# The first layer of the routed experts: clipping and copying out of PSUM on ScalarE instead of VectorE

## Chip, core and metric

One core of a Trainium2 chip runs the whole program once. The metric is device microseconds of one execution. TensorE (PE in the rows) multiplies matrices and writes to PSUM; VectorE (DVE) and ScalarE (ACT) read PSUM; GpSimd (POOL) does elementwise work in SBUF and triggers indirect DMAs.

## What is computed

A decayed linear attention gives x of 3072 tokens by 512. Two dense layers follow. Then comes a mixture of eight experts with fixed capacity: a greedy routing gives every expert exactly 384 tokens, and each expert applies two matrices with a clip at zero between them.

```python
logits = x @ w_gate
flat = logits.flatten()
order = np.argsort(-flat)
...
for e in range(E):
    mask = assigned == e
    h = np.maximum(x[mask] @ w1[e], 0.0)
    out[mask] = h @ w2[e]
```

The change is about `np.maximum(x[mask] @ w1[e], 0.0)`, the expert's first layer.

## The kernel before

Matrices are split into two float16 parts, a high part and the rest, and a product is made of three matmuls (high by high, high by rest, rest by high). So a first-layer result is needed three times: in float32, rounded to float16 (the high part), and as the difference of the two (the rest).

The experts run one after the other in `expert(r)`, r from 0 to 7. The first layer has 8 groups (`f`); a group is 12 matmuls of 128x384 into one PSUM bank. The banks come in turn from `ps_any()`: two called `ph` and two called `px`, four in all, so a bank comes back after four groups. A group leaves PSUM by three instructions: L918 on VectorE scales, clips and writes the float32 copy `hs` (`HS2`, two buffers that lie in the tile `G_67`); L919 on ScalarE rounds `hs` to the high part in `hid` (in `G_68`); L920 on VectorE subtracts for the rest. The second layer follows, three pieces of 24 matmuls of 128x512 into the same banks, each copied out by L936 on ScalarE and scattered to the output by an indirect DMA of GpSimd (L937).

Beside experts 0 to 4 runs the routing, rounds 2 to 6, in `route_round(r)`. A round searches a threshold in five digits. One digit is a loop between two engines: VectorE compares (`against`, L686, result in `ld`), TensorE counts (L729, `pc2x6x` is round 2, step 6), VectorE tests (L731), TensorE sums over partitions (L734, `pn2x7x`), VectorE reduces (L736) and subtracts (L740), and the next compare follows. A round ends with L745, L747, L749, L750 and L751 on VectorE, for which the matmuls L776 (`pp2x10x`) wait. Also beside the experts, `weights(i)` prepares the next expert's matrices: GpSimd triggers the load (L862), ScalarE squares (L868) and writes the high part (L228 in `split`), VectorE writes the rest (L229), after a scale (`se`, L192 to L196) that VectorE makes.

The order on TensorE and ScalarE in this stage is that of the code, woven by a hand-made table of due times (`Weave`, `KN`). The order on VectorE and GpSimd is chosen when the program is built, by a scheduler that works with priorities; `tc.high_priority()` puts the three instructions of a group ahead of others that are ready.

Of the kernel before, what the change touches and what calls it, by code (L numbers as in the profile page):

```python
# [16 lines left out]
AF = mybir.ActivationFunctionType  # L17
OP = mybir.AluOpType
# [7 lines left out]
G = 384  # L26
# [72 lines left out]
def moe_kernel(ctx, tc, qkv, w_in, w_out, w_gate, w1p, w2p,  # L99
               c_mask, c_g, c_gv, c_gs, out, dbg=None):  # L100
    nc = tc.nc
    V, A, P, T, SY = nc.vector, nc.scalar, nc.gpsimd, nc.tensor, nc.sync
# [416 lines left out]
    def mm3(p, pairs, cost):  # L519
        n = len(pairs) * 3  # L520
        piece = PC[0]
        i = 0
        for (sh, sl), (mh, ml) in pairs:
            for a, b in ((sh, mh), (sh, ml), (sl, mh)):
                T.matmul(p, a, b, start=i == 0, stop=i == n - 1)  # L525
                i += 1
                if i % piece == 0 and i < n:
                    yield piece * cost
# [136 lines left out]
    def rt(name, shape, dt=F32, bufs=1):  # L665
        n = int(np.prod(shape))
        w = n if dt in (F32, I32) else (n + 1) // 2
        if name not in views:
            views[name] = []
            for _ in range(bufs):  # L670
                seg = next(x for x in segs if x[1] + w <= x[0].shape[1])
                v = seg[0][:, seg[1]:seg[1] + w]
                seg[1] += w
                v = v if dt == F32 else v.bitcast(dt)[:, :n]
                if len(shape) == 2:
                    v = v.rearrange("p (a b) -> p a b", b=shape[1])
                elif len(shape) == 3:
                    v = v.rearrange("p (a b c) -> p a b c", b=shape[1], c=shape[2])
                views[name].append(v)
        turns[name] = turns.get(name, -1) + 1  # L680
        return views[name][turns[name] % len(views[name])]
# [160 lines left out]
    def ps_any():  # L842
        return next(banks)()
# [63 lines left out]
    def expert(r):  # L907
        W, hid, idx, xt = EWB[r % 2], HID[r % 2], IDX[r], XTE_[r]
        for f in range(NF2):
            if f == 2:  # L910
                RUN.add(r)
            p = ps_any()
            yield from mm3(p[:, :G], [((W[:, 0, k * F + f * 128:k * F + (f + 1) * 128],
                                        W[:, 1, k * F + f * 128:k * F + (f + 1) * 128]),
                                       (xt[:, 0, k], xt[:, 1, k])) for k in range(KD)], 0.163)
            hs = HS2[f % 2]
            with tc.high_priority():
                V.tensor_scalar(hs, p[:, :G], 1.0 / 65536.0, 0.0, op0=OP.mult, op1=OP.max)  # L918
                A.activation(hid[:, 0, f], hs, AF.Copy)  # L919
                V.tensor_tensor(hid[:, 1, f], hs, hid[:, 0, f], op=OP.subtract)  # L920
            yield PC[0] * 0.163
        while r not in SC:
            yield 0.5
        fac = rt("fac", [CPG], bufs=3)
        for c in range(CPG):
            xg = XG[(r % 2) * CPG + c]
            V.tensor_scalar(fac[:, c:c + 1], xg[:, 2 * DM:2 * DM + 2].bitcast(F32), SC[r], None, op0=OP.mult)
        H2.add(r)
        for c in range(CPG):
            p = ps_any()  # L930
            yield from mm3(p, [((hid[:, 0, f, c * C:(c + 1) * C], hid[:, 1, f, c * C:(c + 1) * C]),
                                (W[:, 0, 4096 + f * DM:4096 + (f + 1) * DM], W[:, 1, 4096 + f * DM:4096 + (f + 1) * DM]))
                               for f in range(NF2)], 0.216)
            o = OUTR[(r * CPG + c) % 4]
            with tc.high_priority():
                A.activation(o, p, AF.Copy, scale=fac[:, c:c + 1])  # L936
            s = P.indirect_dma_start(out=out, out_offset=bass.IndirectOffsetOnAxis(ap=idx[:, c:c + 1], axis=0),  # L937
                                     in_=o, in_offset=None)
            for old in scat:
                tc.declare_no_dep(s.ins, old.ins, reason="rows of other tokens")  # L940
            scat.append(s)
            if c == CPG - 1:
                OUT.add(r)
            yield PC[0] * 0.216
# [209 lines left out]
    for r in range(E):  # L1154
        need(lambda: r in XTE and r in SPL)
        wv.run(expert(r))
# [57 lines left out]
```

## Time before, and its profile

| | |
|---|---|
| time, median of 3 runs | 1114.64 us (1114.42 to 1118.55) |
| profiled execution, its own time | 1124.75 us |
| span of that execution | 1123.0 us |
| mean granted TensorE clock | 0.942 |
| busy: PE / DVE / ACT / POOL | 973.1 / 811.1 / 625.3 / 415.1 us |

The span runs from the first to the last instruction of the profiled execution; 1.75 us of its own time lie around it. That execution took 10.1 us (0.9%) more than the median of the three others.

### The profile page before, as it was taken

How to read it: one execution, taken by the hardware profiler on the slowest of the kernel's cores; microseconds unless marked ns; L12 is line 12 of the kernel's file. 1: busy time of each engine (PE TensorE's matmuls, PEld its weight loads, DVE VectorE, ACT ScalarE, POOL GpSimd, SP SyncE). 2: the span in 40 equal slices, each digit the busy share in tenths (PEclk: the TensorE clock that was granted, in tenths of full speed). 3: DMA queues.
4: the chain of work that ended last, by engine and by line, in shares of the span. 5: the costliest groups of instructions: out<-in, count | busy, mean ns of one | idle time of the engine just before them, and what ended most of it. 6: DMA issues, size and time to landing. Idle time of an engine off the chain costs nothing.

```text
span 1123.0 us, 19760 instructions
## 1 busy us (share of the span) xinstructions
PE 973.1 (87%) x7897; PEld 559.5 (50%) x7897; DVE 811.1 (72%) x1815; ACT 625.3 (56%) x925; POOL 415.1 (37%) x301
## 2 busy tenths in 40 slices
PE   3448758898999999999999999997688887979997
PEld 2335434444655555556556555553444544545553
DVE  6899989953676687677767654578779887795641
ACT  4435867563477567567577468126345545455731
POOL 5956364551533463435544514100331211314111
PEclk9959889978999999999999999999699998999999
DMA  9461262156113122131234010062734735726500
GB/s 305 122 187 39 103 178 66 39 118 136 39 38 86 39 62 71 48 85 30 60 101 86 11 38 1 20 207 104 160 108 140 219 100 148 217 86 212 183 29 29
DMA packets 108813, 113.66 MB, mean 101 GB/s; under 512 B 92464, under 2 KB 92592, under 8 KB 106672
## 3 DMA queue, kind: packets, MB, share of 16 engines
q1 hardware_dynamic: 102576, 66.24, 23.3%
q0 software_dynamic: 6144, 46.15, 11.9%
q8 instruction: 62, 1.02, 0.4%
q14 instruction: 31, 0.25, 0.1%
HBM read 77.50 MB, written 13.64 MB: 81 GB/s over the span
## 4 chain that ended last, share of the span: by engine, by line
PE 48%; DVE 24%; issue 15%; POOL 6%; ACT 3%; DMA 2%; another core or an unknown queue 0%; POOLq 0%; SPq 0%; ACTq 0%; DVEq 0%
PE px L525 20%; PE ph L525 19%; DVE WOUT L229 2%; DVE WIN L229 2%; DVE ld L686 2%; PE py L434 2%; DVE RAW L571 1%; POOL out_dram L937 1%; DVE ld L373 1%; POOL amt L406 1%; DVE G L918 1%; DVE RAW L555 1%; PE pa L397 1%; DVE WOUT L249 1%; DMA xt<-yh 1%
## 5 line engine op out<-in xcount | busy, mean ns | idle before, releaser
L525 PE MATMUL ph<-xt,WIN 128*128 128x384 f16 x1728 | 331.1, 333 | 7.9 <-DVE RAW L555 3.6
L525 PE MATMUL px<-WOUT,G 128*128 128x512 f16 x1248 | 314.4, 387 | 0.6 <-DVE WOUT L229 0.6
L525 PEld LDWEIGHTS <-WIN 128*128 128x128 f16 x1920 | 186.4, 100 | 147.9 <-issue 22.4
L525 PEld LDWEIGHTS <-G 128*128 128x128 f16 x1728 | 166.7, 100 | 184.3 <-issue 18.3
L577 POOL TENSOR_TENSOR G<-RAW,G 128x1536 f16<-128x1536 f32 (+1 forms) x32 | 99.5, 3109 | 101.7 <-DVE G L574 88.8
L406 POOL TENSOR_TENSOR amt<-amt 128x512 f16<-128x512 f32 x40 | 55.7, 1394 | 124.4 <-DVE amt L403 108.2
L555 DVE TENSOR_SCALAR RAW<-ph 128x384 f32<-128x384 f32 x124 | 68.0, 550 | 42.0 <-PE ph L525 41.5
L562 ACT ACTIVATE RAW<-RAW,zt,ch 128x1536 f32<-128x1536 f32 x32 | 53.3, 1665 | 52.2 <-DVE RAW L555 48.2
L325 ACT ACTIVATE junk<-ld 128x512 bf16<-128x512 f32 x63 | 39.4, 626 | 62.0 <-DMA ld<-in_qkv_dram 61.1
L919 ACT ACTIVATE G<-G 128x384 f16<-128x384 f32 x64 | 33.0, 519 | 72.5 <-DVE G L918 72.4
L571 DVE TENSOR_TENSOR RAW<-RAW 128x1536 f32<-128x1536 f32 (+1 forms) x33 | 60.0, 1817 | 15.5 <-ACT RAW L570 15.4
L868 ACT ACTIVATE junk<-RAW 128x1024 bf16<-128x1024 f32 x64 | 67.1, 1048 | 6.1 <-DMA RAW<-in_w1p_dram,MASK 5.4
L862 POOL DMA_INDIRECT RAW<-in_w1p_dram,MASK x8 | 8.3, 1041 | 164.9 <-issue 55.2
L223 POOL TENSOR_TENSOR RAW<-ld,RAW 128x512 f16<-128x512 f32 x34 | 45.7, 1358 | 49.9 <-ACT RAW L222 45.0
L228 ACT ACTIVATE WOUT<-RAW,se 128x1024 f16<-128x1024 f32 x32 | 35.7, 1137 | 39.6 <-DVE se L195 39.6
L400 DVE TENSOR_TENSOR amt<-pa,MASK 128x512 f32<-128x512 f32 x38 | 26.1, 687 | 37.8 <-PE pa L399 33.4
L525 PEld LDWEIGHTS <-WOUT 128*128 128x128 f16 x384 | 37.7, 101 | 26.1 <-issue 3.7
L525 PE MATMUL px<-WIN,G 128*128 128x512 f16 x192 | 45.6, 389 | 2.9 <-ACT G L919 2.2
L570 ACT ACTIVATE RAW<-RAW 128x1536 f32<-128x1536 f32 (+1 forms) x33 | 47.7, 1445 | 0.4
L223 POOL TENSOR_TENSOR STH<-SC,STH 64x256 f16<-64x256 f32 x34 | 32.1, 945 | 41.7 <-ACT STH L222 38.7
L563 ACT ACTIVATE RAW<-RAW 128x1536 f32<-128x1536 f32 x32 | 47.2, 1475 | 0.3
L228 ACT ACTIVATE WIN<-RAW,se 128x1024 f16<-128x1024 f32 x32 | 35.7, 1137 | 17.1 <-DVE se L195 17.1
(582 smaller groups left out, 2002.8 us busy)
## 6 DMA issues: line engine op xcount, KB each, us to landing
ld<-in_qkv_dram SPq DMA_DIRECT2D x20, 768.0 KB, 4.9
G<-in_w_in_dram SPq DMA_DIRECT2D x8, 1024.0 KB, 7.2
G<-in_w_out_dram SPq DMA_DIRECT2D x8, 1024.0 KB, 5.4
x_rows<-xr SPq DMA_DIRECT2D x24, 256.5 KB, 2.9
G<-in_qkv_dram SPq DMA_DIRECT2D x2, 768.0 KB, 6.4
g_columns<-G SPq DMA_DIRECT2D x1, 1024.0 KB, 8.5
G<-g_columns SPq DMA_DIRECT2D x1, 1024.0 KB
ld<-in_qkv_dram SPq DMA_DIRECT2D x3, 256.0 KB, 4.2
```

The lines of the kernel that those rows point to most:

```text
L223: (V if pool in ("V", "E") else P).tensor_tensor(lo, src, hi, op=OP.subtract)
L228: A.activation(hi, src, AF.Copy, scale=s)
L229: V.scalar_tensor_tensor(lo, src, s, hi, op0=OP.mult, op1=OP.subtract)
L406: (P if mode[1] == "P" else V).tensor_tensor(amh[:, j, 1], am, amh[:, j, 0], op=OP.subtract)
L525: T.matmul(p, a, b, start=i == 0, stop=i == n - 1)
L555: V.tensor_scalar(hs[:, f], p[:, :G], 1.0 / 65536.0, None, op0=OP.mult)
L562: A.activation(th, hs, AF.Tanh, scale=ch[:, q:q + 1], bias=z)
L563: A.activation(th, th, AF.Arctan, scale=-0.5, bias=0.5)
L570: A.activation(th[:, w], th[:, w], AF.Sin, scale=-2.0, bias=math.pi / 2)
L571: (V if hm[1] == 'V' else P).tensor_tensor(th[:, w], th[:, w], hs[:, w], op=OP.mult)
L577: (P if lo == 'P' else V).tensor_tensor(gb[:, 1, o], th[:, w], gb[:, 0, o], op=OP.subtract)
L868: A.activation(junk(1024), RAW[:, o:o + 1024], AF.Square, accum_out=ss[:, j:j + 1])
```

## The change

The first of the three instructions moves from VectorE to ScalarE, and both of ScalarE's now read PSUM: L918 clips straight into the high part in float16, L919 clips once more into the float32 copy. VectorE keeps the subtraction.

```diff
             hs = HS2[f % 2]
             with tc.high_priority():
-                V.tensor_scalar(hs, p[:, :G], 1.0 / 65536.0, 0.0, op0=OP.mult, op1=OP.max)
-                A.activation(hid[:, 0, f], hs, AF.Copy)
+                A.activation(hid[:, 0, f], p[:, :G], AF.Relu, scale=1.0 / 65536.0)
+                A.activation(hs, p[:, :G], AF.Relu, scale=1.0 / 65536.0)
                 V.tensor_tensor(hid[:, 1, f], hs, hid[:, 0, f], op=OP.subtract)
```

On ScalarE the pair L918, L919 stands wherever L919 stood, 64 times, and nothing else moves; the number of table loads is 65 in both programs. TensorE and SyncE have the same rows as before. On GpSimd some output scatters (L937) change places with loads and gathers. VectorE loses 64 instructions, and the scheduler orders the others anew around them. Three places show how.

VectorE in round 2, beside expert 0's first layer, between two counts of TensorE; before (`G_67` holds `hs`, `G_68` holds `hid`):

```order
L731 TENSOR_SCALAR MASK<-pc2x6x 64x8
L229 SCALAR_TENSOR_TENSOR WOUT<-RAW,se_8832,WOUT 128x1024
L918 TENSOR_SCALAR G_67<-ph 128x384
L736 TENSOR_REDUCE MASK<-pn2x7x 128x1
L740 SCALAR_TENSOR_TENSOR MASK<-MASK 128x192
L918 TENSOR_SCALAR G_67<-px 128x384
L920 TENSOR_TENSOR G_68<-G_67,G_68 128x384
L686 TENSOR_TENSOR ld<-MASK,ld 128x24x64
L920 TENSOR_TENSOR G_68<-G_67,G_68 128x384
L731 TENSOR_SCALAR MASK<-pc2x8x 64x8
```

and now:

```order
L731 TENSOR_SCALAR MASK<-pc2x6x 64x8
L736 TENSOR_REDUCE MASK<-pn2x7x 128x1
L740 SCALAR_TENSOR_TENSOR MASK<-MASK 128x192
L686 TENSOR_TENSOR ld<-MASK,ld 128x24x64
L920 TENSOR_TENSOR G_68<-G_67,G_68 128x384 x2
L731 TENSOR_SCALAR MASK<-pc2x8x 64x8
```

The weight instruction L229 and both L918 have left the way to the compare L686; the subtractions L920 follow it. (An L229 stands further ahead now, before L736 of `pn2x5x`.)

VectorE at the end of round 5, beside expert 3's first layer, before:

```order
L736 TENSOR_REDUCE MASK<-pn5x9x 128x1
L920 TENSOR_TENSOR G_68<-G_67,G_68 128x384
L918 TENSOR_SCALAR G_67<-px 128x384
L745 SCALAR_TENSOR_TENSOR MASK<-pn5x9x,MASK,ld 128x8
L229 SCALAR_TENSOR_TENSOR WIN<-RAW,se_10461,WIN 128x1024
L918 TENSOR_SCALAR G_67<-ph 128x384
L920 TENSOR_TENSOR G_68<-G_67,G_68 128x384
L747 TENSOR_REDUCE MASK<-MASK 128x1
L229 SCALAR_TENSOR_TENSOR WIN<-RAW,se_10461,WIN 128x1024
L920 TENSOR_TENSOR G_68<-G_67,G_68 128x384
L749 TENSOR_SCALAR MASK<-MASK 128x24
```

and now:

```order
L736 TENSOR_REDUCE MASK<-pn5x9x 128x1
L229 SCALAR_TENSOR_TENSOR WIN<-RAW,se_10461,WIN 128x1024
L745 SCALAR_TENSOR_TENSOR MASK<-pn5x9x,MASK,ld 128x8
L920 TENSOR_TENSOR G_68<-G_67,G_68 128x384
L747 TENSOR_REDUCE MASK<-MASK 128x1
L229 SCALAR_TENSOR_TENSOR WIN<-RAW,se_10461,WIN 128x1024
L749 TENSOR_SCALAR MASK<-MASK 128x24
```

The two L918 are gone from this chain, and of three L920 one is left in it; both L229 have stayed.

VectorE in round 6, beside expert 4's first layer, before:

```order
L731 TENSOR_SCALAR MASK<-pc6x6x 64x8
L229 SCALAR_TENSOR_TENSOR WOUT<-RAW,se_10945,WOUT 128x1024
L736 TENSOR_REDUCE MASK<-pn6x7x 128x1
L920 TENSOR_TENSOR G_68<-G_67,G_68 128x384
L740 SCALAR_TENSOR_TENSOR MASK<-MASK 128x192
L918 TENSOR_SCALAR G_67<-px 128x384
L920 TENSOR_TENSOR G_68<-G_67,G_68 128x384
L686 TENSOR_TENSOR ld<-MASK,ld 128x24x64
```

and now:

```order
L731 TENSOR_SCALAR MASK<-pc6x6x 64x8
L229 SCALAR_TENSOR_TENSOR WOUT<-RAW,se_10945,WOUT 128x1024
L736 TENSOR_REDUCE MASK<-pn6x7x 128x1
L920 TENSOR_TENSOR G_68<-G_67,G_68 128x384
L740 SCALAR_TENSOR_TENSOR MASK<-MASK 128x192
L229 SCALAR_TENSOR_TENSOR WOUT<-RAW,se_10945,WOUT 128x1024
L920 TENSOR_TENSOR G_68<-G_67,G_68 128x384
L686 TENSOR_TENSOR ld<-MASK,ld 128x24x64
```

Here L918 is gone from ahead of the compare L686, but a second L229 has come in its place; it stood behind the compare before.

## Rows read from the trace of the kernel before

**Rows 1.** The page: busy time, share of the span and instructions of each engine.
```profile
PE 973.1 (87%) x7897; PEld 559.5 (50%) x7897; DVE 811.1 (72%) x1815; ACT 625.3 (56%) x925; POOL 415.1 (37%) x301
```

**Rows 2.** Stretches: length, busy PE, PEld, DVE, ACT, POOL; PEclk; DMA share, GB/s.
```profile
800.00:998.00 198.00, 173.45 (x1467) 95.53 (x1467) 165.00 (x501) 103.64 (x159) 38.91 (x34) 0.96 0.53 151
...
1014.00:1115.00 101.00, 100.86 (x566) 53.42 (x563) 47.85 (x90) 50.55 (x79) 18.97 (x18) 1.00 0.39 120
```

**Rows 3.** Waits of PE in 800 to 998: us, times, longest.
```profile
PE pp5x10x L776 <- DVE MASK L751: 2.8, 1, 2.8
...
PE pc5x4x L729 <- DVE ld L686: 2.4, 1, 2.4
PE pn4x5x L734 <- DVE MASK L731: 2.0, 1, 2.0
...
PE pc4x8x L729 <- DVE ld L686: 1.5, 1, 1.5
...
PE pc2x8x L729 <- DVE ld L686: 1.3, 1, 1.3
...
PE pp3x10x L776 <- DVE MASK L751: 1.0, 1, 1.0
...
PE pc3x6x L729 <- DVE ld L686: 0.3, 1, 0.3
```

**Rows 4.** PE in order of time, at the end of expert 4's first layer.
```profile
1004.96 0.66 PE L525 MATMUL px<-WIN,G 128*128 128x512 f16 x2 [2.20 <-ACT G L919]
```

**Rows 5.** Groups of DVE in 800 to 998: busy us, mean ns | idle before.
```profile
L229 DVE SCALAR_TENSOR_TENSOR WOUT<-RAW,se,WOUT 128x1024 f16<-128x1024 f32 x20 | 25.5, 1276 | 2.0 <-ACT WOUT L228 2.0
L920 DVE TENSOR_TENSOR G<-G,G 128x384 f16<-128x384 f32 x39 | 21.4, 550 | 0.3
...
L918 DVE TENSOR_SCALAR G<-px 128x384 f32<-128x384 f32 x20 | 11.0, 552 | 4.9 <-PE px L525 4.8
```

**Rows 6.** Groups of ACT in the same stretch.
```profile
L919 ACT ACTIVATE G<-G 128x384 f16<-128x384 f32 x39 | 20.3, 520 | 51.0 <-DVE G L918 50.9
```

**Rows 7.** Line L557 (an ACT copy from PSUM in an earlier phase): ns min/median/max.
```profile
L557 ACT ACTIVATE RAW<-ph x4: 471/491/492, 155.9 to 172.3; 128x384 f32<-128x384 f32 x4
```

**Rows 8.** DVE in order of time, expert 0's first layer, round 2.
```profile
813.58 0.54 DVE L918 TENSOR_SCALAR G<-ph 128x384 f32<-128x384 f32 x1
814.05 0.14 DVE L736 TENSOR_REDUCE MASK<-pn2x7x 128x1 f32<-128x8 f32 x1
...
815.54 0.55 DVE L920 TENSOR_TENSOR G<-G,G 128x384 f16<-128x384 f32 x1
816.01 0.95 DVE L686 TENSOR_TENSOR ld<-MASK,ld 128x1536 bf16<-128x1536 bf16 x1
```

**Rows 9.** DVE, end of round 5.
```profile
943.79 0.17 DVE L736 TENSOR_REDUCE MASK<-pn5x9x 128x1 f32<-128x8 f32 x1
...
947.50 1.27 DVE L229 SCALAR_TENSOR_TENSOR WIN<-RAW,se,WIN 128x1024 f16<-128x1024 f32 x1
...
949.60 0.24 DVE L751 SCALAR_TENSOR_TENSOR MASK<-MASK 128x24 bf16<-128x24 bf16 x1
```

**Rows 10.** ACT, expert 4's first layer.
```profile
980.35 1.15 ACT L228 ACTIVATE WOUT<-RAW,se 128x1024 f16<-128x1024 f32 x1 [3.68 <-DVE se L195]
981.41 0.51 ACT L919 ACTIVATE G<-G 128x384 f16<-128x384 f32 x1
981.82 1.13 ACT L228 ACTIVATE WOUT<-RAW,se 128x1024 f16<-128x1024 f32 x1
```

**Rows 11.** DVE, the same place: the compare that PE waits for.
```profile
984.64 0.95 DVE L686 TENSOR_TENSOR ld<-MASK,ld 128x1536 bf16<-128x1536 bf16 x1
```

**Rows 12.** Two stretches with a lower granted clock (columns as in rows 2).
```profile
950.00:954.00 4.00, 4.00 (x18) 1.99 (x17) 3.55 (x19) 1.47 (x3) 0.98 (x1) 0.60 0.31 55
1004.00:1015.00 11.00, 9.32 (x52) 3.92 (x53) 8.10 (x17) 6.79 (x10) 5.21 (x4) 0.69 0.21 48
```

**Rows 13.** PE, one group of expert 7, whose first layer runs undisturbed.
```profile
1085.51 2.11 PE L525 MATMUL px<-xt,WOUT 128*128 128x384 f16 x12
```

## The prediction

> **What bounds the kernel now.** I read the page first [rows 1]: TensorE is busy for 87% of the span, VectorE for 72%, ScalarE for 56%. A mean over the span says little of this change, which touches the eight experts alone, so I cut the expert stage with the view of stretches [rows 2]. From 1014 to 1115 us TensorE is busy for 100.86 of 101 us at full clock: nothing that another engine does faster can shorten that part, though TensorE could be made to wait anew. From 800 to 998 us, where the routing runs beside experts 0 to 4, TensorE is idle for 198.00 - 173.45 = 24.6 us, and VectorE is busy for 165 of 198. At 1004.96 TensorE waits another 2.2 us [rows 4]. So the change plays for at most some 27 us of idle TensorE, and for what a low clock costs after such waits.
>
> The waits say who makes TensorE idle [rows 3]. Nearly all of it is VectorE. Four waits are for L751, the end of a routing round, from 2.8 to 1.0 us, 8.0 in sum. Seven are for the compare L686 beside a first layer, from 1.5 to 0.3 us, 7.6 in sum. `pc5x4x` waits 2.4 us for a compare beside a second layer. The rest is short, with one exception: `pn4x5x` waits 2.0 us for a test (L731) that VectorE began late though it had nothing else to do. I cannot put that on VectorE's load, and leave it as it is.
>
> **The change, part by part.** *VectorE loses L918.* Each takes 0.55 us [rows 5]; the next instruction starts 0.47 us after it began (813.58 to 814.05) [rows 8], so each one gone frees 0.47 us of the queue. 40 of the 64 stand between 800 and 998 (the group with `px` is one half of them): 18.8 us of a queue that is busy for 165. The 24 behind stand where TensorE does not wait and are worth nothing.
>
> *ScalarE gains a read of PSUM.* The trace has the same shape with an immediate scale in line L557: 0.49 us [rows 7]; L919 from SBUF is 0.52 [rows 6]. One L919 begins and the next L228 follows 0.41 us later (981.41 to 981.82) [rows 10], so I take 0.39 us of the queue for each new one. A clip out of PSUM is not in ScalarE's rows. Bounds: 0.47, L557's shortest, and 0.55, what VectorE's clip takes; I take 0.49, the row with the same engine, source and shape. ScalarE's added time is 40 x 0.39 = 16 us in the stretch, on 103.64 of 198 busy.
>
> On this the Trainium skill speaks against the change: the page "ScalarE: Activation LUTs", section "Rules for kernel authors", sends relu and max to VectorE, as the engine that is faster per element. The rows differ for this shape, float32 out of PSUM: 0.55 us on VectorE against 0.49 on ScalarE. By the rule the move would cost more than it frees, and the time would be that of the first rival below.
>
> *ScalarE waits for TensorE instead of VectorE.* L919 waited 50.9 us in this stretch for L918 [rows 6]. Now the pair waits for the group's last matmul, and VectorE's queue no longer delays it. Behind it stand L228 and L868 of the next weights, which come a little earlier too. No table load is added (65 in both programs). The high part, which TensorE needs first, is written by the first of the two.
>
> *The queue of VectorE is ordered anew.* This decides the sum. I walked three places.
>
> Round 2, beside expert 0. Before, L736 started at 814.05 behind L918, and the compare at 816.01 behind L918 and L920 [rows 8]; the count after it waited 1.3 us [rows 3]. In the new order the two L918, the L920 and an L229 are gone from between: more than 1.3 us even of the three 0.47 alone. This wait goes: -1.3.
>
> End of round 5. From L736 at 943.79 to the end of L751 at 949.84 [rows 9] VectorE needs 6.05 us: 3 x 0.47 for L920, 2 x 0.47 for L918, 2 x 1.2 for L229, the rest for the short chain. TensorE was through 2.8 us before that, at 947.1. The new order has two L229 and one L920 between, four times 0.47 = 1.9 us less, and the idle time before an L918 goes: L751 ends near 947.8, and 0.7 of 2.8 us are left. -2.1.
>
> Round 6, beside expert 4. Here a second L229 comes ahead of the compare, against one L918 gone, and it has to wait for its L228. On ScalarE an L228 (1.06 us) and a pair (0.8, before 0.41) alternate [rows 10]; with the scale 0.4 sooner the third L228 ends near 984.8. L229 and L920 follow (1.2 + 0.47), and the compare starts near 986.6 instead of 984.64 [rows 11]. The wait grows by about 1.3, since the test before it is 0.7 late as well and holds TensorE there: +2.0 together.
>
> The others I walked the same way, without rows here. The four round ends lose 6.1 of their 8.0 us. Of the seven compares beside first layers four have one L229 more ahead of them in the new order, two the same number and one has one less: in sum -1.5 of 7.6 (bounds: -7.6 if all go, +5 if each of the four grows by one L229). `pc5x4x` has one L229 less: -1.2. The start of round 3 has one L918 less: -0.5. At 1004.96 TensorE waits 2.2 us [rows 4] for the high part of expert 4's last group, which stands on ScalarE behind an L228 that waits for VectorE's scale; VectorE is three L918 earlier there, and now writes nothing between: -1.4. Sum: -10.7 us.
>
> *The clock.* After such waits the granted clock is lower: 0.60 from 950 to 954, 0.69 from 1004 to 1015 [rows 12]. That costs 0.40 x 4.0 = 1.6 and 0.31 x 9.3 = 2.9 us of TensorE's time; over 800 to 998 the mean is 0.96 [rows 2], 0.04 x 173 = 6.9 us. Which of these vanish hangs on single microseconds. Bounds 0 and -9.8; I take a third, -3.
>
> *GpSimd's order.* Output scatters change places with loads; the gathers of an expert's tokens stand a whole expert ahead of their use in both orders, and that covers it. If the cover went, a gather's trigger would be late by one scatter, about a microsecond.
>
> *From 1014 on.* ScalarE has 50.55 us of work in 101 [rows 2]; 24 pairs add 9. A bank is needed again three groups later, and a group takes 2 us [rows 13], so a pair may be 6 us late before TensorE waits. By the walk it is 1 to 4 us late. Nothing.
>
> The sum on the profiled execution is 1124.75 - 13.7 = 1111.0. The median of the other runs is 10.1 us lower, so part of the waits in this trace are not in those runs, and my walks allow for no accidental stall. I carry 70% over: 1114.6 - 9.6 = **1105.0 us**.
>
> **Rivals.**
>
> *ScalarE gives the time back (about 1114 us).* L920 now comes after two instructions of ScalarE, each pair behind an L228 (1.06 us) or an L868. VectorE runs its rows in their order, so an L920 that waits for ScalarE holds the routing chain behind it. Before, this cost 0.3 us in the stretch [rows 5]. If each of 40 L920 waits 0.25 us more, 10 us are gone and no gain is left. For it: a pair is 0.4 us longer than L919. Against it: the pair begins sooner, by what the 50.9 us of waits for L918 were. This is where the rule of the Trainium skill named above would lead.
>
> *The new order makes it slower (about 1121 us).* The place in round 6 is the model: an L229 ahead of the compare costs 2 us there. If all four such places cost that (+8) and the round ends gain nothing, with two of them losing an L229's 1.2 (+2), against 3 to 4 us saved elsewhere, the sum is +6 or 7. It decides from the point where the L229 that moved ahead cost more than the freed 18.8 us of queue return on the path. For it: four of seven compares do get one more. Against it: the L918 that are gone, 0.47 us each, stood in the same stretches of the queue.
>
> *A bank comes late (about 1114 us).* ScalarE may stand at an L228 that waits for a scale, 3.68 us [rows 10], while the group in front of it is done. Before, VectorE emptied the bank meanwhile. In round 6 the lag becomes 3.3 us, under the 6 that are free. If it grew by another 5 at each of the five experts, stalls of 2 us would take the gain.
>
> *Everything falls into place (about 1096 us).* All waits for VectorE but the odd one go (-21), the clock stays up (-6), and 70% of it shows.
>
> **How the numbers follow.** What a measurement of this kernel can tell from no change is about 0.5%, 5.6 us: faster is below 1109.1, slower above 1120.2. The forecast has 0.55, everything in place 0.08, ScalarE giving it back 0.19, the late bank 0.05, the new order 0.13. Faster 0.63, same 0.24, slower 0.13. The range leaves out 0.08 below and 0.12 above: 1097 to 1117.
>
> **What would show it.** L918 as an instruction of ScalarE of about 0.49 us, and 40 instructions fewer on VectorE from 800 to 1000. TensorE idle in that stretch for about 14 us instead of 24.6. Waits for L751 of a microsecond or less; a longer wait of `pc6x8x`; the wait near 1005 at about 0.8. L920 idle for ScalarE under 3 us. The prediction is wrong if L920 waits 10 us or more for L919, if the compares wait longer in most rounds, or if TensorE waits for a bank that ScalarE has not read.

## The result, and the profile after

The changed kernel takes 1102.84 us in the median of 4 runs (1102.40 to 1103.25), beside 1114.53 us of the kernel before (4 runs, 1113.72 to 1118.55) on the same chip: a ratio of 0.989, 95% interval 0.987 to 0.991. In a second set of runs, on a chip where the kernel before took 1118.09 us, it was 1102.47 us, a ratio of 0.986 (0.981 to 0.990). The profiled execution took 1103.10 us, its span is 1101.3 us. Medians and ratios leave out executions more than 1.5% above the fastest of their kernel; only `free` below has such, four of twelve, and its profile is of one of them.

The page answers to [rows 1]. VectorE has 64 instructions fewer, ScalarE 64 more, and TensorE is busy for a little less time with the same matmuls:

```profile
PE 966.6 (88%) x7897; PEld 559.9 (51%) x7897; DVE 783.0 (71%) x1751; ACT 646.3 (59%) x989; POOL 416.8 (38%) x301
```

The stretches answer to [rows 2] (length, busy PE, PEld, DVE, ACT, POOL; PEclk; DMA share, GB/s). From 800 to 998 us TensorE is idle for 198.00 - 183.88 = 14.1 us, where it was 24.6. The two stretches do not hold the same work: the last L776 of the routing, that of round 7, starts at 980.5 us now, at 998.0 before, and the new stretch holds about 100 matmuls more. Up to that L776, from 800 to 980.5 us, TensorE is idle for 180.50 - 167.82 = 12.7 us. The undisturbed part begins earlier, and TensorE is still busy for all of it:

```profile
800.00:998.00 198.00, 183.88 (x1566) 101.78 (x1565) 163.08 (x511) 127.34 (x214) 51.57 (x40) 0.98 0.56 167
...
992.00:1093.00 101.00, 101.00 (x567) 53.59 (x565) 38.36 (x69) 58.38 (x104) 21.10 (x19) 1.00 0.39 123
```

The waits of PE from 795 to 1012 us (us, times, longest) answer to [rows 3]. Of four waits for L751 two are left, 2.0 us in sum; `pc5x4x` waits 0.2 us. Two compares wait clearly longer than they did: `pc6x8x`, 2.4 us instead of 1.3, with the test before it (`pn6x7x`, 0.8), and `pc6x2x`, 1.2 instead of 0.3. (The longest in this window, `pc2x2x`, lies ahead of 800 us; it is 4.4 us, 4.5 before.) Two rows of the kernel before, then the new waits:

```profile
PE pp4x10x L776 <- DVE MASK L751: 2.6, 1, 2.6
...
PE pc6x8x L729 <- DVE ld L686: 1.3, 1, 1.3
```

```profile
...
PE pc6x8x L729 <- DVE ld L686: 2.4, 1, 2.4
PE pp4x10x L776 <- DVE MASK L751: 1.2, 1, 1.2
PE pc6x2x L729 <- DVE ld L686: 1.2, 1, 1.2
...
PE pc2x6x L729 <- DVE ld L686: 0.9, 1, 0.9
PE pp5x10x L776 <- DVE MASK L751: 0.8, 1, 0.8
PE px L525 <- DVE G L920: 0.8, 1, 0.8
PE pn6x7x L734 <- DVE MASK L731: 0.8, 1, 0.8
...
PE pc4x8x L729 <- DVE ld L686: 0.7, 1, 0.7
...
PE pc3x6x L729 <- DVE ld L686: 0.6, 1, 0.6
PE pc3x8x L729 <- DVE ld L686: 0.5, 1, 0.5
...
PE pc5x4x L729 <- DVE ld L686: 0.2, 1, 0.2
```

ScalarE's groups from 800 to 998 us answer to [rows 6] (busy us, mean ns | idle before). A clip out of PSUM takes 0.49 us. Ahead of the first of a pair ScalarE is idle for 14.9 + 8.5 = 23 us, nearly all for TensorE; ahead of the second hardly ever:

```profile
L919 ACT ACTIVATE G<-ph 128x384 f32<-128x384 f32 x20 | 9.8, 490 | 0.0
L918 ACT ACTIVATE G<-px 128x384 f16<-128x384 f32 x20 | 9.8, 488 | 14.9 <-PE px L525 14.8
...
L918 ACT ACTIVATE G<-ph 128x384 f16<-128x384 f32 x20 | 9.7, 486 | 8.5 <-PE ph L525 8.2
```

VectorE's L920 in the same stretch answers to its row in [rows 5]. It now waits 4.4 us for ScalarE, 0.3 before:

```profile
L920 DVE TENSOR_TENSOR G<-G,G 128x384 f16<-128x384 f32 x40 | 22.1, 551 | 4.4 <-ACT G L919 4.4
```

VectorE in order of time (start, us) at the three places of the prediction answers to [rows 8, 9, 11]. In round 2 the compare follows L740 with nothing between, and its count does not wait. The end of round 5 takes 932.54 - 928.70 = 3.84 us from the start of L736 to that of L751, 949.60 - 943.79 = 5.81 before. In round 6 an L229 and an L920 stand between L740 and the compare:

```profile
814.11 0.42 DVE L740 SCALAR_TENSOR_TENSOR MASK<-MASK 128x192 bf16<-128x192 bf16 x1
814.56 0.96 DVE L686 TENSOR_TENSOR ld<-MASK,ld 128x1536 bf16<-128x1536 bf16 x1
...
928.70 0.17 DVE L736 TENSOR_REDUCE MASK<-pn5x9x 128x1 f32<-128x8 f32 x1
...
932.54 0.24 DVE L751 SCALAR_TENSOR_TENSOR MASK<-MASK 128x24 bf16<-128x24 bf16 x1
...
966.44 1.28 DVE L229 SCALAR_TENSOR_TENSOR WOUT<-RAW,se,WOUT 128x1024 f16<-128x1024 f32 x1
967.63 0.55 DVE L920 TENSOR_TENSOR G<-G,G 128x384 f16<-128x384 f32 x1
968.10 0.95 DVE L686 TENSOR_TENSOR ld<-MASK,ld 128x1536 bf16<-128x1536 bf16 x1
```

The place of [rows 4] on PE, at the end of expert 4's first layer, waits 0.64 us instead of 2.20:

```profile
985.92 0.60 PE L525 MATMUL px<-WIN,G 128*128 128x512 f16 x2 [0.64 <-ACT G L918]
```

### The profile page after: what moved, and what is told of

The parts are those of the page before. It is cut to its first block, busy times and chain, and to the rows that moved or that the text cites. A ratio compares the mean times of both kernels' runs of the same rounds, so it can differ in the third digit from the quotient of the medians.

```text
span 1101.3 us, 19732 instructions
## 1 busy us (share of the span) xinstructions
PE 966.6 (88%) x7897; PEld 559.9 (51%) x7897; DVE 783.0 (71%) x1751; ACT 646.3 (59%) x989; POOL 416.8 (38%) x301
## 4 chain that ended last, share of the span: by engine, by line
PE 49%; DVE 26%; issue 11%; POOL 5%; ACT 5%; DMA 3%; POOLq 0%; SPq 0%; ACTq 0%; DVEq 0%
PE px L525 19%; PE ph L525 19%; DVE WOUT L229 2%; DVE ld L686 2%; PE py L434 2%; DVE WIN L229 2%; DVE RAW L571 1%; DMA xt<-yh 1%; DVE ld L373 1%; DVE G L920 1%; DMA ld<-in_qkv_dram 1%; DVE RAW L555 1%; POOL amt L406 1%; PE pa L397 1%; POOL out_dram L937 1%
## 5 line engine op out<-in xcount | busy, mean ns | idle before, releaser
L920 DVE TENSOR_TENSOR G<-G,G 128x384 f16<-128x384 f32 x64 | 35.4, 554 | 31.5 <-ACT G L919 31.5
L937 POOL DMA_INDIRECT out_dram<-G,MASK x18 | 24.9, 1383 | 58.4 <-ACT G L936 53.7
```

## The experiments

**The two kernels again.** `again` is the kernel before, `after2` the changed one. The first profile of before had been 10 us above the other runs, and it had to be seen which of its waits are in every run.

> The kernel before, once more. If the 10 us by which the profiled execution of before was above the other runs were accidental stalls, this profile has an own time of 1112 to 1116 us, and rounds 3 to 5 (from one L776 to the next) take about 40 us each instead of 42.6 to 42.9. If they belong to the kernel's profile, the own time is again near 1124 us and the rounds are as long as they were. Time against the kernel before: no difference, within 0.2%.

`again` took 1118.46 us (12 runs), 1.0005 of the kernel before (0.9991 to 1.0018); its profiled execution 1118.83 us, between the two cases that were expected; its rounds 3 to 5 take 39.9, 40.9 and 43.1 us. Its waits of PE for L751 and L686 are those of [rows 3], nearly all to within 0.2 us:

```profile
PE pp5x10x L776 <- DVE MASK L751: 2.8, 1, 2.8
PE pp4x10x L776 <- DVE MASK L751: 2.8, 1, 2.8
...
PE pc4x8x L729 <- DVE ld L686: 1.5, 1, 1.5
```

`pc5x4x` (1.6 us, 2.4 in the first profile) differs more, and the one wait that could not be explained, `pn4x5x` 2.0 us, is gone. So the waits for VectorE belong to the kernel, and the odd one, as far as two profiles can tell, to that one execution.

> The changed kernel once more, so that the other runs stand beside it on one chip: 0.986 to 0.991 of the kernel before, and the same waits of TensorE as in its first profile, within 0.5 us each.

`after2`: 1102.47 us (6 runs, 1101.39 to 1105.24), 0.9857 (0.9813 to 0.9902), own time 1102.29; `pc6x8x` 2.4, `pp4x10x` 1.2, `pp5x10x` 0.8, as in the first profile. The kernel before spreads over 13 us in the same set (1113.32 to 1126.53, 23 runs), the changed one over 4.

**Which experts pay.** `early` makes the change for experts 0 to 4, `late` for 5 to 7 (the edit of `early`, against the changed kernel; `late` has `r >= 5`); up to expert 4 VectorE's order is that of the changed kernel in the one, that of the kernel before in the other.

```diff
-                A.activation(hid[:, 0, f], p[:, :G], AF.Relu, scale=1.0 / 65536.0)
+                A.activation(hid[:, 0, f], p[:, :G], AF.Relu, scale=1.0 / 65536.0) if r < 5 else V.tensor_scalar(hs, p[:, :G], 1.0 / 65536.0, 0.0, op0=OP.mult, op1=OP.max)
-                A.activation(hs, p[:, :G], AF.Relu, scale=1.0 / 65536.0)
+                A.activation(hs, p[:, :G], AF.Relu, scale=1.0 / 65536.0) if r < 5 else A.activation(hid[:, 0, f], hs, AF.Copy)
```

> The change for experts 0 to 4 alone; experts 5 to 7 as before. Theory (all of the gain is made beside the routing; the 24 clips behind it are worth nothing): 1101.5 to 1104.5 us, as the changed kernel. Rival (the last three experts gain or lose by it too): off the changed kernel by more than 2 us.

> The change for experts 5 to 7 alone; experts 0 to 4 as before, with the order of VectorE as before up to there. Theory: 1113 to 1116 us, as the kernel before. Rival (the last part has a share of the gain): below 1112 us.

`early`: 1101.87 us, 0.9855 (0.9831 to 0.988). `late`: 1118.53 us, 1.000 (0.9983 to 1.0017), beside 1117.37 of the kernel before in the same set (the band expected for `late`, 1113 to 1116, lies round the first set's 1114.53). The gain is made beside the routing; for the 24 clips behind it neither run shows any.

**ScalarE's waits or VectorE's queue.** Two things changed at once for experts 0 to 4: VectorE has less to do, and ScalarE no longer waits for it. `free` was to take only the second; its edit is shown against the changed kernel.

```diff
-                A.activation(hid[:, 0, f], p[:, :G], AF.Relu, scale=1.0 / 65536.0)
-                A.activation(hs, p[:, :G], AF.Relu, scale=1.0 / 65536.0)
+                V.tensor_scalar(hs, p[:, :G], 1.0 / 65536.0, 0.0, op0=OP.mult, op1=OP.max)
+                A.activation(hid[:, 0, f], p[:, :G], AF.Relu, scale=1.0 / 65536.0)
```

> Only half of the change: the high part is clipped out of PSUM by ScalarE, but VectorE keeps its clip into the float32 copy. ScalarE waits for no VectorE instruction here, and VectorE's queue is as full as before. Theory (the freed queue of VectorE pays): at most 3 us of the 11.7 appear, 1111.5 to 1116 us, and the four waits for L751 stay at 6 us or more in sum. Rival (what pays is that ScalarE no longer waits 51 us for VectorE): nearly the whole gain, 1102 to 1106 us.

1116.44 us (8 runs), 0.9999 (0.9971 to 1.0027): no gain. But it does not tell the two apart, since ScalarE waited as before. In its groups of ACT L919 reads PSUM and still waits 44 us for VectorE's L918, whose result it does not use (50.9 and 45.0 us for the same pair in the two profiles of the kernel before):

```profile
L919 ACT ACTIVATE G<-px 128x384 f16<-128x384 f32 x20 | 9.8, 488 | 28.3 <-DVE G L918 28.3
L919 ACT ACTIVATE G<-ph 128x384 f16<-128x384 f32 x19 | 9.2, 485 | 16.3 <-DVE G L918 16.0
```

So the built program puts the two engines' reads of one bank in order. The Trainium skill states why one would (page "PSUM — Partial Sum Buffer", section "PSUM bank collisions raise a hardware error"): two engines must not access one bank in the same partitions at once, reads with reads included. The wait in the row agrees; no run here shows a collision.

So three others were made. `load` and `twice` fill VectorE's queue again while ScalarE waits for TensorE alone: `load` with an instruction that reads the float32 copy, `twice` with the subtraction made a second time. `tiny` was to do the opposite: a VectorE instruction of one column stands ahead of ScalarE's clip.

```diff
# load
+                V.tensor_scalar(hid[:, 1, f], hs, 1.0, 0.0, op0=OP.mult, op1=OP.max)
                 V.tensor_tensor(hid[:, 1, f], hs, hid[:, 0, f], op=OP.subtract)
# twice
                 V.tensor_tensor(hid[:, 1, f], hs, hid[:, 0, f], op=OP.subtract)
+                V.tensor_tensor(hid[:, 1, f], hs, hid[:, 0, f], op=OP.subtract)
# tiny
+                V.tensor_scalar(hid[:, 0, f, :1], p[:, :1], 1.0, 0.0, op0=OP.mult, op1=OP.max)
                 A.activation(hid[:, 0, f], p[:, :G], AF.Relu, scale=1.0 / 65536.0)
```

> The changed kernel with one more VectorE instruction in each group, of the removed one's size (128x384, from the float32 copy in SBUF into the place of the rest, which the subtraction then overwrites). VectorE's queue is as full as before the change, but ScalarE waits for TensorE alone. Theory (the freed queue of VectorE pays): the gain is lost again, 1111 to 1118 us. Rival (what pays is that ScalarE no longer waits for VectorE): 1101 to 1105 us.

> The opposite: in each group one VectorE instruction of a single column reads the bank first, and ScalarE's first clip waits for it. VectorE's queue is nearly as free as in the changed kernel (0.1 us for each instead of 0.47), but ScalarE waits for VectorE again, 30 us or more in the stretch of experts 0 to 4. Theory: 1101 to 1107 us, most of the gain stays. Rival: 1111 to 1117 us.

`load`: 1108.11 us, 0.9909 (0.9882 to 0.9936), between the two bands that were expected. Its filler was shorter than planned, 0.35 us where L918 took 0.55:

```profile
L920 DVE TENSOR_SCALAR G<-G 128x384 f16<-128x384 f32 x40 | 14.2, 354 | 3.2 <-ACT G L919 3.1
```

`tiny`: 1100.70 us, 0.9843 (0.9817 to 0.9869). ScalarE waits 28 us for VectorE again (the waits of ACT from 800 to 998 us), and nothing of the gain is lost:

```profile
ACT G L918 <- DVE G L918: 27.9, 23, 2.9
```

But those 28 us are only 5 more than the 23 that ScalarE waits for TensorE at the same place in the changed kernel. `tiny` does not bring back the 45 to 51 us of the kernel before.

> The changed kernel with the subtraction L920 made twice, so that VectorE's queue gets back 0.47 us for each group (the filler of the run before was only 0.35 us long, not 0.55); ScalarE still waits for TensorE alone. Theory (the freed queue of VectorE pays): at least two thirds of the gain are lost, above 1112 us where the kernel before takes 1117. Rival (the gain comes from ScalarE's side, or from the luck of a new order): below 1107 us.

`twice`: 1119.09 us (12 runs), 1.0009 (0.9977 to 1.0041). With two L920 of 0.55 us for each group all of the gain is gone, although ScalarE's clips wait for TensorE alone here, 25.6 us. The group of DVE, the waits of ACT and of PE, and the stretch of round 5:

```profile
L920 DVE TENSOR_TENSOR G<-G,G 128x384 f16<-128x384 f32 x78 | 42.1, 552 | 7.9 <-ACT G L919 7.4
```

```profile
ACT G L918 <- PE px L525: 17.3, 13, 3.0
...
ACT G L918 <- PE ph L525: 8.3, 4, 2.8
```

```profile
PE pp4x10x L776 <- DVE MASK L751: 4.2, 1, 4.2
PE pc6x0x L729 <- DVE ld L686: 2.9, 1, 2.9
```

```profile
900.40:944.10 43.70, 39.25 (x313) 20.75 (x313) 34.26 (x106) 24.32 (x42) 9.34 (x8) 0.89 0.52 151
```

The long waits are back for L751 (4.2 us) and for the compares, and round 5 has a granted clock of 0.89. `twice` keeps what the change did for ScalarE, its wait for TensorE alone, and has no gain: ScalarE's freedom does not make the gain by itself, and VectorE's freed queue is needed for it. `tiny` adds that a wait of ScalarE for a short VectorE instruction costs nothing. The opposite of `twice`, VectorE freed while ScalarE waits for it as long as before, was not run.

**The order or what stands in it.** Each of these kernels has an order of VectorE of its own. `low` and `before_low` take L920 out of the high priority, in the changed kernel and in the kernel before; in `low` the other engines keep their orders.

```diff
             with tc.high_priority():
                 ...
-                V.tensor_tensor(hid[:, 1, f], hs, hid[:, 0, f], op=OP.subtract)
+            V.tensor_tensor(hid[:, 1, f], hs, hid[:, 0, f], op=OP.subtract)
```

> The changed kernel with L920 taken out of the high priority, so that the compares and the ends of the routing rounds go ahead of it on VectorE; nothing else changes its place on any other engine. Theory (what is left of the waits is VectorE's queue ahead of the compares and the round ends): 2 to 5 us less than the changed kernel. Rival (a late L920 holds the two float32 copies, ScalarE's second clip waits for them and TensorE for a bank, or the second layer for its rest): no gain, or slower by 2 us or more.

> The kernel before with the same edit, L920 out of the high priority, and L918 still on VectorE. It tells the order of VectorE's queue from what stands in it. Theory (the load itself, 0.47 us of each L918, is what costs): a third of the gain or less, 0.995 of the kernel before or above. Rival (a better order alone would have done it): 0.991 or below.

`before_low`: 1115.91 us, 0.9977 (0.995 to 1.0003): this other order alone is worth 0.2%, at most 0.5. The waits for L751 still make 5.7 us, of 8.0 (PE, 800 to 1004 us; `pp5x10x` is 1.6):

```profile
PE pp4x10x L776 <- DVE MASK L751: 2.2, 1, 2.2
...
PE pp6x10x L776 <- DVE MASK L751: 1.9, 1, 1.9
```

`low`: 1101.68 us, 0.9845 (0.9801 to 0.9889), 0.8 us below `after2`, less than the runs can tell; the 2 to 5 us of the theory did not come. The wait of `pc6x8x` is 1.2 us there instead of 2.4, but the second layer now waits for its rest, 4.6 us in all where the changed kernel waits 0.8. So the rival was right in that:

```profile
PE px L525 <- DVE G L920: 2.7, 2, 1.9
PE ph L525 <- DVE G L920: 1.9, 2, 1.2
```

**Room on ScalarE and on GpSimd.** `third` adds a third clip of ScalarE to each group, into a scratch tile; `pool` moves L920 to GpSimd.

```diff
# third
                 A.activation(hs, p[:, :G], AF.Relu, scale=1.0 / 65536.0)
+                A.activation(junk(G), p[:, :G], AF.Relu, scale=1.0 / 65536.0)
# pool
-                V.tensor_tensor(hid[:, 1, f], hs, hid[:, 0, f], op=OP.subtract)
+                P.tensor_tensor(hid[:, 1, f], hs, hid[:, 0, f], op=OP.subtract)
```

> The changed kernel with a third ScalarE clip out of PSUM in each group, into a scratch tile that nobody reads: 0.39 us more of ScalarE's queue, 16 us over experts 0 to 4, and L920 waits for none of it directly. Theory (ScalarE has room, 54 to 70 us idle in 198): up to 3 us more than the changed kernel, 1101 to 1106 us. Rival (ScalarE is about to become the bound, through the weights L228 that come later): 1109 us or more.

> The changed kernel with the subtraction L920 on GpSimd instead of VectorE: VectorE's queue loses another 0.47 us in each group. Theory (VectorE's queue makes the remaining waits beside the routing): 1094 to 1100 us. Rival (GpSimd takes over a microsecond for it, its triggers of loads and gathers come late, or the rest of a group comes too late for the second layer): 1103 us or more.

`third`: 1098.26 us, 0.982 (0.9793 to 0.9846). ScalarE is busy for 144.61 of 198 us and nothing is lost. It came out lower than the changed kernel, which was not expected; the two were not run in one set, and the intervals overlap. Its stretches show where: round 6 takes 39.9 us at full clock, 42.4 at 0.96 in the changed kernel.

```profile
800.00:998.00 198.00, 186.86 (x1616) 104.57 (x1615) 162.65 (x514) 144.61 (x259) 53.70 (x43) 0.99 0.59 175
...
929.50:969.40 39.90, 36.53 (x325) 20.35 (x325) 32.76 (x103) 29.35 (x54) 11.47 (x8) 1.00 0.54 166
```

`low`, with another order again, has 39.70 us for the same round. That the order in round 6 makes these 2.5 us is likely; no run changes that place alone.

`pool`: 1111.15 us, 0.9939 (0.9919 to 0.9958), not the 1094 to 1100 of the theory: about half of the gain is lost, though 40 more instructions have left VectorE in that stretch. Two costs show in the rows, and their shares were not separated: GpSimd needs 1.1 us for the subtraction, and VectorE's own instructions grew, an L229 from 1.28 to 1.42 us and the compare from 0.95 to 1.09.

```profile
L920 POOL TENSOR_TENSOR G<-G,G 128x384 f16<-128x384 f32 x40 | 44.1, 1104 | 43.2 <-ACT G L919 42.9
```

```profile
L229 DVE SCALAR_TENSOR_TENSOR WIN<-RAW,se,WIN 128x1024 f16<-128x1024 f32 x16 | 22.5, 1424 | 0.8 <-ACT WIN L228 0.8
L686 DVE TENSOR_TENSOR ld<-MASK,ld 128x1536 bf16<-128x1536 bf16 x15 | 16.3, 1089 | 0.3
```

## Why the prediction was right, and where it was off

**VectorE's queue.** Right. `twice` gives all of the gain back, `load` about a third of it, `tiny` nothing, and `early` and `late` put it beside experts 0 to 4, as said.

**The walk.** Right in most of its places, and in the one that was to get worse. The four round ends lost 6.0 us (forecast 6.1). The seven compares went from 7.6 to 5.1 us, with 0.8 us more for the test ahead of one of them: 1.7 less (1.5). In round 6 the compare waits 1.1 us longer and the test 0.8, 1.9 in sum (2.0), behind the L229 that came ahead. `pc5x4x` lost 2.2 us (1.2), the wait near 1005 1.6 us (1.4). Not foreseen was `pc6x2x`, 1.2 us instead of 0.3, and `pp4x10x` keeps 1.2 us, over the microsecond that was named. Idle TensorE from 800 to 998 is 14.1 us (about 14), but that agreement is partly luck. Up to the last L776 it fell by 24.6 - 12.7 = 11.9 us, and of the -10.7 the -1.4 at 1004.96 lay behind that stretch. Some short waits that the walk left alone went too, among them the odd `pn4x5x`. The 40 instructions fewer on VectorE cannot be read off the fixed stretch either (511 in it, 501 before), since it holds more work.

**ScalarE's side.** The clip takes 0.49 us, the value taken. The first rival had L920 waiting 10 us or more; it waits 4.4 us, over the 3 that were named. Half of it, 2.23 us, is one L920 at 806.44 us, and no wait of TensorE for the test L731 behind it is in the list. `third` bounds the rival: 40 more clips on ScalarE cost nothing, though they stand behind the one that L920 waits for. The rule named for it (the Trainium skill, page "ScalarE: Activation LUTs", section "Rules for kernel authors") gives its reason for bf16. For float32 out of PSUM it did not hold here: 0.49 us on ScalarE, 0.55 on VectorE.

**The late bank** did not come: no wait of PE for a bank that ScalarE has not read is among its waits (the one for L918, 0.64 us at 985.92, is for the high part), and from 992 to 1093 us TensorE is busy for 101.00 of 101 us. **The new order** was no rival in the end; it cost about 2 us in round 6 and is worth a few microseconds from one order to the next, against 12 to 16 of the load. GpSimd's order, which the prediction put at nothing, was not tested by itself: it differs in three places between the two kernels, and that of `twice` is the order of the kernel before again but for two places. The long waits that went were, but for the one near 1005, waits for VectorE.

**The clock** is the term that was mis-sized most: -3 us, taken as a third of its bound of 9.8. The second profile of the kernel before shows it best, since it lacks the accidental wait. The stretches run from one L776 to the next, rounds 3 to 6, and from round 7's to the end; first the kernel before, then the changed kernel (columns as above):

```profile
819.90:859.80 39.90, 35.95 (x320) 20.10 (x319) 36.67 (x111) 24.35 (x38) 10.63 (x8) 1.00 0.54 166
859.80:900.70 40.90, 36.62 (x317) 20.24 (x317) 36.12 (x110) 23.88 (x38) 8.23 (x8) 0.96 0.67 161
900.70:943.80 43.10, 37.87 (x313) 20.40 (x313) 35.52 (x108) 23.19 (x36) 9.07 (x8) 0.92 0.56 153
943.80:986.00 42.20, 38.19 (x323) 20.87 (x323) 35.63 (x106) 22.71 (x36) 9.45 (x8) 0.96 0.53 156
...
991.90:1117.00 125.10, 114.06 (x634) 58.93 (x633) 61.89 (x140) 58.67 (x89) 24.38 (x21) 0.95 0.36 116
```

```profile
821.10:859.10 38.00, 36.03 (x322) 20.06 (x320) 33.36 (x103) 26.10 (x45) 10.32 (x8) 1.00 0.57 174
859.10:896.40 37.30, 35.15 (x317) 19.72 (x316) 32.16 (x98) 26.76 (x47) 11.73 (x8) 1.00 0.61 177
896.40:932.80 36.40, 34.47 (x311) 19.45 (x311) 31.53 (x100) 24.30 (x41) 8.77 (x8) 1.00 0.61 182
932.80:975.20 42.40, 37.80 (x325) 20.76 (x325) 33.18 (x106) 25.91 (x44) 11.24 (x8) 0.96 0.50 156
...
980.50:1101.30 120.80, 111.31 (x636) 58.19 (x633) 49.72 (x111) 66.69 (x114) 23.71 (x21) 0.98 0.36 117
```

The matmuls are the same. In round 4 TensorE's busy time falls from 36.62 to 35.15 us as the granted clock goes from 0.96 to 1.00, in round 5 from 37.87 to 34.47 with 0.92 to 1.00, in round 3 it stays, at 1.00 in both. With round 6 and the end (0.95 to 0.98) that makes -7.9 us of busy time, against -3. The idle time of these five stretches goes from 28.5 to 20.1 us; with round 2 ahead of them (16.0 to 14.2) that is -10.2, and the idle part of the sum was -10.7. (Beside the first profile, on which the sum was made, the same stretches give -8.1 us of busy and -14.4 of idle time.) The two make -18.1, and the spans differ by 15.7: in this execution of the changed kernel the stretch of round 2 begins 2.9 us later (776.9 us, 774.0 before), and the stretches left out make the rest.

**The 70%** had a reason that did not hold. It assumed that a part of the waits in the first profile is not in the other runs; `again` has nearly all of them, only the odd one is gone and `pc5x4x` shorter. Its size is not decided: the full sum of -13.7 would have given 1100.9, 1.9 us below the 1102.84 of the first set, as 1105.0 is 2.2 above it; measured is -11.7 there and -15.6 in the second set. That 1105.0 came so close to the first set is in part luck, since the clock term was too small and the 2.9 us ahead of round 2 were in no term.

## What to carry to other kernels

What an instruction cost here, on an engine that serves a search loop, went by its place in the queue ahead of the loop's next step and not by its share of the span: 0.47 us for each of 40 instructions made 12 to 16 us of 1115, and the 24 like them behind the loop made nothing. Walk the new order at the places where the bound engine waits, and look for what has moved ahead, not only for what is gone. Count the clock along with the idle time: as the waits went, the granted clock rose in rounds 4 and 5 and at the end, and that was worth 7.9 us of busy time beside 10.2 of idle time.

## What the runs showed of the hardware

- A clip out of PSUM in float32, 128x384, takes 0.49 us on ScalarE and 0.55 us on VectorE; from SBUF into float16 VectorE's takes 0.35 us.
- The subtraction of two SBUF operands takes 1.10 us on GpSimd and 0.55 us on VectorE, and VectorE's instructions beside it get longer, by 11 to 14% in the rows shown. The Trainium skill has both: the factor of about two (page "GPSIMD Engine Reference", section "4.1 Engine selection") and a port pair that GpSimd shares with VectorE's two-input instructions, held by one of them at a time (page "SBUF — State Buffer", section "Who interferes with whom"). The longer rows agree; no run here shows the port itself.
- `twice` and the kernel before in its set spread over 12 us and more from run to run (1112.29 to 1128.83 in 12 runs, 1113.32 to 1126.53 in 23); kernels with the queue freed over 1 to 4 us in 4 to 6 runs (1100.16 to 1102.60 for `low`). But `again`, the kernel before on another chip, spread over 3.7 us only in 12 runs, so a full queue does not always bring the spread. The two profiles of the kernel before differ in the rounds in which the granted clock is low (round 3 in the first, round 5 the more in the second). That this makes the spread was not tested.
